# A written order that reaches through three units of the second block, with two places for values

## The chip, the cores and the metric

The kernel runs on one core of a Trainium2 chip. The metric is the device time of one execution in microseconds (us); the kernel before takes 1208.21 us, the median of three runs. Of the core's engines, TensorE (PE in the rows) multiplies matrices, VectorE (DVE), ScalarE (ACT) and GpSimd (POOL) work element by element, and SyncE (SP) issues the transfers (DMA). Each engine takes its instructions in the order of the program; between engines they wait on semaphores.

## The reference

Attention over windows with memory keys, then two expert layers on its output, all float32:

```python
for c in range(nc):                                   # 24 chunks of 32 queries, 4 batches, 8 heads
    k_full = concat([mem_k, k[:, :, l_start:r_end]])  # 8 memory keys, up to 16 + 32 + 8 of the window
    scores = scale * q_c @ k_full.T
    a = exp(scores - max(scores)); a = a / (sum(a) + 1e-09)
    out[:, :, c_start:c_end] = a @ v_full
x = out as 3072 tokens x 512
h = x @ w_in;  x = (h * sigmoid(1.702 * h)) @ w_out                       # 512 -> 2048 -> 512
g = x @ w_gate; x = (g * sigmoid(g) * (x @ w_val)) @ w_out2               # 512 -> 1536 -> 512
```

The weights arrive as float64 and are made into float32 on the chip.

## The kernel before, in words

The 3072 tokens are six blocks of 512. A block's attention is four groups of 128 tokens. A group is a chain: scores on TensorE (`sc`), maximum and difference on DVE (`mx`), exponential on ACT (`ex`), sum on DVE (`sm`), a guard on ACT (`ra`), reciprocal and weighing on DVE (`wg`), four transposes on TensorE (`te`, "turn"), two copies on ACT into the tile `ebd` (`ec`), 16 value products on TensorE (`pv`) against the group's value tile, and a copy of the output on ACT (`xf`), which SP stores to DRAM (`st`). Names in brackets are those of the written order.

Every float32 operand of an expert product is kept as two parts, high and low, and a product is three TensorE passes. A unit of the first expert layer covers 256 of 2048 hidden columns. It takes seven products of the tokens with prepared weights (each six matmuls of 256 columns, the helper `product`), sums and copies of parts of them on DVE and ACT, an activation on two banks `ps_a` and `ps_b`, and four "down" products (six matmuls of 512 columns each, `down`) into four long-lived banks `y`. The tokens enter as seven operands (class `Tokens`): sums and differences of quarters of the tile `xf` (`ts`), then a high part by ACT (`tc`) and a low part by DVE or POOL (`tl`). Two of the differences are written back into `xf`.

The weights come as raw 512 KB tiles (`ldw`, three places `raw` and four more lent at the start), are joined into float32 (`pr` on ACT, `cs`, `ct` on DVE), summed in quarters on POOL (`sumA`, `sumB`) and split into two parts (ACT then POOL). A unit needs four raw tiles: two of input weights, two of output weights.

The first block runs two units in a plain form (`ua`, `ub`: 12 matmuls of 512 columns for each of four halves), and all later blocks of the first pass four units in the form above. What is left of the units follows in a second pass, then the second expert layer.

What sets the order. The five queues of the start are written by hand: the table `OPENING` (before: line 796) lists steps by name, and every step issues its instructions on its engines and SP in that order. Before, it ends with the operands of the second block's tokens. From there on the loop (line 865) issues one unit after another: inside `unit` (line 448) the attention of the next block stands at fixed places (`PLACES`), and the weights' conversions are spread by `pace`. Before, there is one value tile `vm` for the attention outside the table and two `ebd` tiles.

Of the kernel before, what the change touches and what calls it, by code (L numbers as in the profile page):

```python
# [19 lines left out]
P = 128  # L20
# [37 lines left out]
def tile_attention_moe_moe(  # L58
# [40 lines left out]
    vm = apool.tile([P, HP, 4, D], F32, name="vm")  # L99
    ebd = [apool.tile([P, HP, 4, 2, CH], F32, name=f"ebd{i}") for i in range(2)]  # L100
# [12 lines left out]
    def load_kv(n, g):  # L113
        if n == "v":
            nc.sync.dma_start(out=vm, in_=vg[g])
# [31 lines left out]

    def st_weigh(g):
        r, e = rt.pop(g), et[g]
        nc.vector.reciprocal(r, r)  # L150
        nc.vector.tensor_tensor(e, e, r.unsqueeze(2).to_broadcast([P, H, KW]), op=ALU.mult)
# [6 lines left out]

    def keep_e(g, ps, engs):
        for e, copy in enumerate(engs):  # L160
            r = slice(64 * e, 64 * e + 64)
            copy(ebd[g % 2][r, :, :, e, :], ps[r].rearrange("p a (c q) -> p a c q", c=4))  # L162

    def values(g, ps, v):
        ps = ps.rearrange("p (a q) -> p a q", a=KC)
        for a in range(0, HP, 2):
            for c in range(4):
                for j in range(2):
                    nc.tensor.matmul(  # L169
                        ps[64 * j : 64 * j + 64, a : a + 2, CH * c : CH * c + CH],  # L170
                        v[:, a + j, c, :],
                        ebd[g % 2][:, a + j, c].rearrange("p e q -> p (e q)"),
                        start=True,
                        stop=True,
                    )
        return ps
# [13 lines left out]
    def st_scores(g):  # L190
        ps = bank("ps_s").rearrange("p (h k) -> p h k", h=H)
        q = qt.pop(g)
        for hp in range(HP):
            for c in range(4):
                r = slice(CH * c, CH * c + CH)
                nc.tensor.matmul(  # L196
                    ps[r, 2 * hp : 2 * hp + 2, :], q[:, hp, r], kbd[:, :, hp, c, :], start=True, stop=True
                )
        if g + 1 < NG:
            load_qk(g + 1)  # L200
        exponents(g, ps)
        st_exp(g)
# [71 lines left out]
    nraw, bits = [len(AT)], {}  # L274
# [80 lines left out]
    ready = {(1, u) for u in range(PLAIN)}  # L355

    def all_weights():
        for ph in (1, 2):
            for u in range(PLAIN if ph == 1 else 0, UNITS[ph]):
# [21 lines left out]
    class Tokens:  # L381


        def __init__(self, src, engs):
            n = BLK // 2
            self.b11, self.b12 = src[:, 0:2, :n], src[:, 0:2, n:]
            self.b21, self.b22 = src[:, 2:4, :n], src[:, 2:4, n:]
            self.engs = engs
            self.ops = [None] * 7

        def sum(self, k):
# [5 lines left out]
            elif k == 1:  # L397
                eng.tensor_sub(self.b12, self.b12, self.b11)
            elif k == 2:
                self.t2 = cpool.tile([P, 2, BLK // 2], F32, tag="t2", name="t2")  # L400
                eng.tensor_add(self.t2, self.t3, self.b11)  # L401
            else:
                eng.tensor_sub(self.b11, self.b21, self.t2)  # L403

# [153 lines left out]
    def down(ph, b, u, first, last, gs, base, dst, d, scale, passes=PASSES):  # L558
# [16 lines left out]
        if ends:  # L575
            del acc[d]
            if base is not None:
                t = base[d]
                nc.vector.scalar_tensor_tensor(t, y, scale, t, op0=ALU.mult, op1=ALU.add)
            else:  # L580
                t = opool.tile([P, 512], F32, tag="o", name="o")
                if d % 2 == 0:
                    nc.scalar.activation(t, y, AF.Copy, scale=scale)
                else:
                    nc.vector.tensor_scalar_mul(t, y, scale)
            nc.sync.dma_start(out=dst(b, d), in_=t)
# [49 lines left out]
    EC = [(nc.scalar.copy,) * 2] * 8  # L636
    firsts, pairs, at, tok = [[None] * 2 for _ in range(PLAIN)], [], {}, []

    def load_q(g):
        if g % GRP < 2:  # L640
# [27 lines left out]
    def scores_first(g):  # L668
        ps = ps_s.tile([P, 2 * BLK], F32, tag="s", name="ps_k")[:, HALF : HALF + BLK]
# [9 lines left out]
    def exponents_first(g):  # L679
        exponents(g, at.pop(("k", g)).rearrange("p e a k -> p (e a) k"), True)  # L680
# [4 lines left out]
    def values_first(g):  # L685
        at["x", g] = values(g, bank("ps_v"), v_open[g % 3])
# [25 lines left out]

    def sums_of(u):
        return quarters(raws[2 * u + 1]), bits[2 * u], bits[2 * u + 1]

    def pair_of(u, i):
        return quarters(raws[2 * u + 1])[:, 2 * i : 2 * i + 2].rearrange("p s n -> p (s n)")

    def split_b(u):
        wt[1, u, "a21"] = bpool.tile([P, 2, HALF], F32R, tag="b", name="a21")  # L720
        split_hi(wt[1, u, "a21"], bits[2 * u + 1][:, :HALF], 0, HALF)
# [20 lines left out]

    def tokens():
        if not tok:
            tok.append(Tokens(xf[1], [G, G, G, V, G, V, V, V, G, V, V]))
# [14 lines left out]
        "ra": st_guard,  # L760
        "wg": st_weigh,
        "te": turned,
        "ec": lambda g: keep_e(g, at.pop(("e", g)), EC[g]),
# [7 lines left out]
        "wa": lambda u: new_split((1, u, "a"), bits[2 * u]),  # L771
        "wal": lambda u: split_lo(wt[1, u, "a"], bits[2 * u]),
        "sumA": lambda u: first_sums(*sums_of(u)),
        "sumB": lambda u: second_sums(*sums_of(u)),
        "wv": lambda u: new_split((1, 0, "v"), bits[2 * u + 1][:, HALF:], u * HALF, HALF),
        "wvl": lambda u: split_lo(wt[1, 0, "v"], bits[2 * u + 1][:, HALF:], u * HALF, HALF),
        "wb": split_b,
        "wbl": lambda u: split_lo(wt[1, u, "a21"], bits[2 * u + 1][:, :HALF], 0, HALF),
# [4 lines left out]
        "wo": lambda o: new_split((1, o // 2, o % 2), bits[4 + o]),  # L783
        "wol": lambda o: split_lo(wt[1, o // 2, o % 2], bits[4 + o]),
# [6 lines left out]
        "dn": down_first,  # L791
        "tc": lambda k: tokens().split_hi(k),
# [4 lines left out]
        z0 tb0 z1 ldk0 ldq0 ldk1 ldq1 ldq2 ldk2 ldk3 ldw0 ldq3 ldw1 sc0 ldv0 mx0 ldq4 sc1 ldv1 ldk4 ex0 mx1 z2  # L797
        sc2 ldq5 sm0 ex1 ldk5 sm1 ra0 wg0 ra1 pr0 ldq6 wg1 te0 ldq7 sc3 mx2 ec0 te1 cs0 pr1 ldv2 mx3 ex2 pv0
        ldk6 ec1 cs1 ldk7 sm2 ex3 ct0 pv1 ldv3 hi0 sm3 ra2 wa0 ldw2 wg2 sc4 ra3 wal0 xf1 ldw3 wg3 xf0 te2 hi1
        xl0 sc5 mx4 st0 ec2 ldv4 te3 ldw4 mx5 ec3 xl1 pv2 ldq8 ct1 ex4 ex5 sm4 sumA0 ldw5 wb0 sm5 wv0 ra4 ldw6  # L800
        sc6 wvl0 wg4 xf2 wbl0 ra5 hi2 wg5 pv3 ldw7 sumB0 hiA0 mx6 te5 hi3 te4 xl2 xf3 ldv5 ua0 xl3 pr2 ec5 cs2
        ua1 loA0 ct2 ldv6 pr3 st3 wa1 cs3 ub0 ec4 ct3 wal1 st2 ub1 th0 sumA1 st1 wb1 gt0 wv1 ldk8 ua2 th1 sumB1
        gc0 gt1 pv4 pr4 rs0 wbl1 gc1 ub2 cs4 ldv7 pr5 wvl1 ct4 xf4 ua3 cs5 wo0 st4 ct5 hiB0 wol0 sc7 rs1 wo1 ub3
        th2 mx7 wol1 hiB1 pv5 ex6 gt2 loB1 ex7 dn0 sm6 xf5 loB0 sm7 gc2 st5 dn1 tc0 rs2 ldw8 ra7 tl0 th3 wg7 tc1
        dn2 gt3 ra6 tl1 pr6 wg6 gc3 te7 dn3 pr7 cs6 rs3 ec7 cs7 te6 ct7 ec6 pv7 ct6 wo3 pv6 xf7 wol3 xf6 st7 wo2
        ts0 st6 ldv8 hiA1 ts2 ts1 ts3 tc3 wol2 tl3 tc2 tc5 tl2 tl5 tc4 tc6 tl4 tl6 loA1
# [4 lines left out]
    for i in range(SPARE):  # L811
        give_w(("spare", i))
# [30 lines left out]
    def run(step):  # L843
        for f, g in step:
            f(g)
            if f is st_scores:
                soon.extend([(st_sums, st_guard, g), (st_weigh, g)])
# [17 lines left out]
    for n, (ph, b, ua, ub) in enumerate(seq):  # L865
# [4 lines left out]
        steps = attention(b + 1) if attends else []  # L870
        base = None
        for u in range(ua, ub):
# [6 lines left out]
            places = PLACES[u - ua] if n and attends else ()  # L879
# [18 lines left out]
            if n:  # L898
# [20 lines left out]
        if not n:  # L919
            pends[0] = None  # L920
# [53 lines left out]
```

## Time and profile before

| what | before |
|---|---|
| median of 3 runs (lowest, highest) | 1208.21 us (1207.19, 1208.73) |
| the profiled execution, its span | 1204.81 us, 1203.0 us |
| TensorE busy | 1155.2 us, 96% |
| DVE, ACT, POOL busy | 649.2, 566.7, 352.5 us |
| DMA queue of SP, share of 16 engines | 130.05 MB, 34.5% |

The profiled execution is one run; the times in its rows start at its first instruction. A busy share is an average over the whole span, so the stretches have to be looked at one by one. A busy TensorE need not run at its full clock, so the granted clock of a stretch is read with its busy time.

### The profile page before, as it was taken

To read this page: it belongs to the slowest core of one execution; us is meant where nothing else is said; L and a number is where in the kernel's file an instruction comes from. 1 tells how busy PE (TensorE), PEld (TensorE's weight loads), DVE (VectorE), ACT (ScalarE), POOL (GpSimd) and SP (SyncE) were. 2 spreads that over 40 slices of the span, in tenths; PEclk is the share of its full clock that TensorE was granted. 3 is DMA by queue.
4 is the path that set the end of the run, shared out by engine and by line. 5 is a ranking of instruction groups with operands and counts; after the bars stand their busy time and mean duration, and the time that the engine had idled before them with its cause. 6 is when DMAs were issued, how large, how long until landed. Compare 5 with 4: busy or idle time off the path is not lost.

```text
span 1203.0 us, 22302 instructions
## 1 busy us (share of the span) xinstructions
PE 1155.2 (96%) x8908; PEld 1042.7 (87%) x8908; DVE 649.2 (54%) x1117; ACT 566.7 (47%) x1185; POOL 352.5 (29%) x321
## 2 busy tenths in 40 slices
PE   4868899999999999999999999999999999999998
PEld 3757788888889999898998989999998989999997
DVE  6666665575674444443456564444556454454553
ACT  4655555454565544543465553342455443343342
POOL 2653312020455331320245433120255521020110
PEclk9888999999999999999999999999999999999999
DMA  9957363633434324223222331110225120320302
GB/s 309 301 161 196 120 177 104 170 106 114 141 123 124 105 89 140 85 74 106 96 97 88 123 123 36 71 55 17 88 76 168 56 97 10 106 80 27 106 23 84
DMA packets 62920, 131.47 MB, mean 109 GB/s; under 512 B 5728, under 2 KB 26208, under 8 KB 60512
## 3 DMA queue, kind: packets, MB, share of 16 engines
q1 hardware_dynamic: 62816, 130.05, 34.5%
q8 instruction: 70, 1.15, 0.4%
q14 instruction: 34, 0.28, 0.1%
HBM read 98.57 MB, written 31.46 MB: 108 GB/s over the span
## 4 chain that ended last, share of the span: by engine, by line
PE 85%; DMA 4%; DVE 4%; ACT 3%; issue 2%; POOL 1%; SPq 0%; DVEq 0%; ACTq 0%; POOLq 0%
PE y L568 35%; PE ps_a L433 26%; PE ps_c L433 12%; PE ps_b L433 8%; DMA raw<-in_wr 1%; DMA vm<-in_vg 1%; PE ps_o L169 1%; PE ps_s L196 1%; PE ps_u L529 1%; DMA xd<-xf 1%; DMA w<-in_kg 1%; PE ps_t L156 1%; ACT ebd L162 0%; DVE gs L548 0%; DVE b L419 0%
## 5 line engine op out<-in xcount | busy, mean ns | idle before, releaser
L433 PEld LDWEIGHTS ps_a<-b,w 128*128 128x128 f32 x2832 | 385.3, 190 | 50.6 <-ACT p L466 11.4
L433 PE MATMUL ps_a<-b,w 128*128 128x256 f32 x2832 | 398.6, 283 | 16.2 <-ACT p L466 10.1
L568 PE MATMUL y<-gs,w 128*128 128x512 f32 x1152 | 300.4, 396 | 1.0 <-DVE gs L548 0.8
L568 PE MATMUL y<-w,gs 128*128 128x512 f32 x864 | 247.8, 395 | 0.6 <-DVE gs L548 0.5
L568 PEld LDWEIGHTS y<-gs,w 128*128 128x128 f32 x1152 | 204.6, 190 | 37.1 <-DVE gs L548 2.3
L433 PE MATMUL ps_c<-b,w 128*128 128x256 f32 x1224 | 179.1, 282 | 0.0
L433 PEld LDWEIGHTS ps_c<-b,w 128*128 128x128 f32 x1224 | 167.1, 190 | 8.8
L568 PEld LDWEIGHTS y<-w,gs 128*128 128x128 f32 x864 | 144.2, 190 | 14.5 <-DVE gs L548 1.7
L249 POOL TENSOR_TENSOR w<-wf,w 128x512 fp32r<-128x512 f32 (+1 forms) x68 | 78.0, 1148 | 227.3 <-ACT w L246 215.2
L433 PE MATMUL ps_b<-b,w 128*128 128x256 f32 x900 | 135.4, 287 | 1.0 <-DVE e L131 0.5
L433 PEld LDWEIGHTS ps_b<-b,w 128*128 128x128 f32 x900 | 120.7, 193 | 5.8 <-issue 2.1
L536 ACT ACTIVATE g<-ps_b 128x512 f32<-128x512 f32 x72 | 43.0, 598 | 166.0 <-DVE ps_b L491 166.0
L419 DVE TENSOR_TENSOR b<-xl,b 128x512 fp32r<-128x512 f32 x72 | 64.5, 895 | 80.5 <-ACT b L415 80.3
L485 DVE TENSOR_TENSOR ps_a<-m,ps_a 128x256 f32<-128x256 f32 x118 | 50.2, 425 | 105.4 <-PE ps_a L433 99.4
L475 ACT COPY u<-ps_a 128x256 f32<-128x256 f32 x118 | 44.0, 373 | 109.1 <-PE ps_a L433 108.8
L403 POOL TENSOR_TENSOR xl<-xl,t 128x512 f32<-128x512 f32 x18 | 23.3, 1293 | 231.0 <-DVE t L401 229.8
L548 DVE TENSOR_TENSOR gs<-ps_a,gs 128x512 fp32r<-128x512 f32 x118 | 80.9, 686 | 10.4 <-ACT gs L544 10.1
L470 DVE TENSOR_TENSOR ps_b<-p,ps_b 128x256 f32<-128x256 f32 x118 | 50.4, 427 | 60.6 <-PE ps_b L433 55.2
L544 ACT CAST gs<-ps_a 128x512 fp32r<-128x512 f32 x118 | 69.8, 591 | 25.1 <-DVE ps_a L514 15.7
L514 DVE TENSOR_TENSOR ps_a<-g,ps_a 128x512 f32<-128x512 f32 x72 | 50.0, 694 | 46.0 <-PE ps_a L433 45.5
L466 ACT COPY p<-ps_a 128x256 f32<-128x256 f32 x118 | 44.0, 373 | 58.4 <-PE ps_a L433 54.2
L491 DVE TENSOR_TENSOR ps_b<-u,ps_c 128x256 f32<-128x256 f32 x102 | 43.6, 427 | 50.0 <-PE ps_c L433 49.7
(112 smaller groups left out, 1182.4 us busy)
## 6 DMA issues: line engine op xcount, KB each, us to landing
raw<-in_wr SPq DMA_DIRECT2D x49, 512.0 KB, 3.4
xl<-yd SPq DMA_DIRECT2D x12, 1024.0 KB, 4.8
vm<-in_vg SPq DMA_DIRECT2D x19, 512.0 KB, 4.1
kbd<-in_kg SPq DMA_DIRECT2D x32, 256.0 KB, 4.1
raw<-in_wr SPq DMA_DIRECT2D x30, 256.0 KB, 4.2
yp<-o SPq DMA_DIRECT2D x24, 256.0 KB, 3.0
xl<-xd SPq DMA_DIRECT2D x6, 1024.0 KB, 4.8
base<-yp SPq DMA_DIRECT2D x24, 256.0 KB, 3.6
```

The source lines that it names most:

```text
L249: nc.gpsimd.tensor_sub(w[:, 1, o : o + n], f, w[:, 0, o : o + n].bitcast(F32))
L419: self.engs[k].tensor_sub(x[:, 1], self.source(k), x[:, 0].bitcast(F32))
L433: nc.tensor.matmul(ps, w[:, a, o + kc * P : o + kc * P + P], x[:, c, kc, :], start=(start and kc == 0 and (a, c) == PASSES[0]), stop=(kc = ...
L466: nc.scalar.copy(p1, ca[:, :n])
L470: add(cb[:, :n], p1, cb[:, :n])
L475: nc.scalar.copy(u2, ca[:, :n])
L485: add(ca[:, n:], m, ca[:, :n])
L491: add(cb[:, n:], u2, cc)
L514: late[0] = [lambda: nc.vector.tensor_mul(ca, t, ca), lambda: gs.append(cast(ca))]
L544: nc.scalar.copy(x[:, 0], g)
L548: nc.vector.tensor_sub(x[:, 1], g, x[:, 0].bitcast(F32))
L568: nc.tensor.matmul(y, lhs, rhs, start=(first and o == 0 and (a, c) == PASSES[0]), stop=(ends and o == len(gs) - 1 and (a, c) == passes[-1]),)
```

## The change

The table of the written order reaches further. It now also holds the attention of the third block (groups 8 to 11), the first three of the second block's four units, product by product (`qa` to `qg`), with the copies, sums, activations and down products around them, and the conversions of two more units' weights (raw tiles 8 to 15 in addition to 0 to 7). The loop runs only the fourth unit of the second block with its own order, and takes over `late`, the last steps of the third unit.

Values get two places `vm` everywhere, and the next load is asked for two groups ahead; the second `ebd` tile exists only in the lent weight space during the start. The tokens' two differences of the second block go to other tiles (`place`). The reciprocal is a step of its own. The first four raw tiles come in four pieces of 128 partitions instead of two of 64. The first block's down results of both units are summed in the banks and then brought out (`held`, `ev`, `sy`).

```diff
-    vm = apool.tile([P, HP, 4, D], F32, name="vm")
-    ebd = [apool.tile([P, HP, 4, 2, CH], F32, name=f"ebd{i}") for i in range(2)]
+    vm = [apool.tile([P, HP, 4, D], F32, name=f"vm{i}") for i in range(2)]
+    ebd = [apool.tile([P, HP, 4, 2, CH], F32, name="ebd")]
...
+    def st_reciprocal(g):
+        nc.vector.reciprocal(rt[g], rt[g])
...
+    def weights_at(g):
+        return ebd[g % 2 if g < 2 * GRP else 0]
...
     def st_pv(g):
-        ps = values(g, bank("ps_o"), vm)
-        if g + 1 < NG:
-            load_kv("v", g + 1)
+        ps = values(g, bank("ps_o"), vm[g % 2])
+        if g + 2 < NG:
+            load_kv("v", g + 2)
...
+            if i < 2 * PLAIN:
+                src = wr[k].rearrange("(e d) (b a n) -> b e a d n", e=2, b=2, a=2)
+                for j in range(4):
+                    nc.sync.dma_start(out=raws[-1][:, j * P : j * P + P], in_=src[j // 2, j % 2])
+                continue
...
-    need, made = [next(weights)], [20 * PLAIN]
+    need, made = [next(weights)], [40 * PLAIN]
...
             elif k == 1:
-                eng.tensor_sub(self.b12, self.b12, self.b11)
+                b12, self.b12 = self.b12, self.place(self.b12)
+                eng.tensor_sub(self.b12, b12, self.b11)
...
+        def place(self, t):
+            if not self.apart:
+                return t
+            return opool.tile([P, BLK], F32, tag="o", name="t").rearrange("p (k n) -> p k n", k=2)
...
-    v_open = [vm] + [spare[12 + i].bitcast(F32).rearrange("p (a c d) -> p a c d", a=HP, c=4) for i in range(2)]
+    v_open = vm + [spare[12].bitcast(F32).rearrange("p (a c d) -> p a c d", a=HP, c=4)]
+    ebd.append(spare[13].bitcast(F32).rearrange("p (a c e q) -> p a c e q", a=HP, c=4, e=2))
...
+    def down_second(d):
+        down(1, 0, 1, False, True, firsts[1], None, None, d, 0.5, held=full)
...
+    def unit_product(new, out, w, o, k):
+        def f(u):
+            if new:
+                un[u][new] = bank(f"ps_{new}")
+            key, off = ((1, u, w), o) if w != "v" else ((1, u - u % 2, "v"), u % 2 * HALF)
+            product(out(u), wt[key], off, tokens().ops[k], start=out is cb1 and k == 2 or new is not None)
...
-        ts0 st6 ldv8 hiA1 ts2 ts1 ts3 tc3 wol2 tl3 tc2 tc5 tl2 tl5 tc4 tc6 tl4 tl6 loA1
+        ts2 ex9 ts1 hiB1 sm9 pv8 ts3 tc3 loB1 th3 tl3 qa0 ldv10 tc2 dn1 gt3 ra9 tl2 tc5 rc9 cp0 tl5 qb0 gc3 qc0
+        tc4 rs3 qd0 tc6 tl4 wg9 sc10 cu0 tl6 cm0 wa2 qe0 ct7 ldq12 xf8 wal2 qf0 ldk11 ac0 wo3 te9 pr9 st8 ad0
...
+    late[0] = [lambda: unit_rest("b")(2), lambda: unit_gate("a")(2)]
+    late[1] = [lambda: unit_cast("a")(2)]
+    late[2] = [lambda: unit_rest("a")(2)]
...
-            if n:
+            if n == 1 and u < 3:
+                gs = seconds[u]
+            elif n:
```

Three places show how instructions move. The first is TensorE's row between the first block's last down products and the second block's first unit product. `ps_u` are the plain halves, `ps_t` turns, `ps_v` value products, `ps_k` and `ps_s` scores, `y` down products, `ps_a` and `ps_b` unit products. Before:

```order
L568 MATMUL y_910<-gs,w 128x512 x6
L156 MATMUL ps_t<-ident,e 128x128 x4
L169 MATMUL ps_v<-ebd_119,w 64x2x32 x16
L169 MATMUL ps_v<-ebd_118,vm 64x2x32 x16
L433 MATMUL ps_a<-b,w 128x256 x6
L433 MATMUL ps_b<-b,w 128x256 x6
L433 MATMUL ps_a<-b,w 128x256 x6
L196 MATMUL ps_s<-kbd,q 32x128 x16
```

Now:

```order
L590 MATMUL y_943<-gs,w 128x512 x6
L174 MATMUL ps_v<-w,vm_118 64x2x32 x16
L201 MATMUL ps_s<-kbd,q 32x128 x16
L158 MATMUL ps_t<-ident,e 128x128 x4
L551 MATMUL ps_u<-xh,a_635 128x512 x2
L551 MATMUL ps_u<-xh,w 128x512 x2
L551 MATMUL ps_u<-xh,a_635 128x512 x2
L551 MATMUL ps_u<-xh,w 128x512 x2
L551 MATMUL ps_u<-xl,a_635 128x512 x2
L551 MATMUL ps_u<-xl,w 128x512 x2
L174 MATMUL ps_v<-ebd,vm_117 64x2x32 x16
L455 MATMUL ps_a<-b,w 128x256 x6
```

The unit products used to start behind all down products of the first unit and all eight value products. Now the ninth group's scores and value product, a turn and the last plain half stand ahead of the first unit product, and down products follow behind it.

The second place is TensorE's row in the second and third unit of the second block. Before:

```order
L169 MATMUL ps_o<-ebd_119,vm 64x2x32 x16
L433 MATMUL ps_a<-b,w 128x256 x12
L433 MATMUL ps_b<-b,w 128x256 x6
L568 MATMUL y_1449<-gs,w 128x512 x6
L433 MATMUL ps_a<-b,w 128x256 x6
L156 MATMUL ps_t<-ident,e 128x128 x4
L196 MATMUL ps_s<-kbd,q 32x128 x16
L433 MATMUL ps_b<-b,w 128x256 x6
```

Now:

```order
L455 MATMUL ps_a<-b,w 128x256 x6
L455 MATMUL ps_b<-b,w 128x256 x6
L455 MATMUL ps_a<-b,w 128x256 x6
L455 MATMUL ps_b<-b,w 128x256 x6
L455 MATMUL ps_a<-b,w 128x256 x6
L455 MATMUL ps_b<-b,w 128x256 x6
L455 MATMUL ps_a<-b,w 128x256 x12
L455 MATMUL ps_b<-b,w 128x256 x6
L455 MATMUL ps_a<-b,w 128x256 x6
```

Before, a down product, a turn or scores stand between unit products; now the seven products of the second unit stand one behind the other and the third unit's follow.

The third place is SP's row around the fourth and fifth group's values (`vm` or `w` from `in_vg`); `in_kg` are keys, `in_qg` queries, `in_wr` raw weights, `xd` the store of the attention's output. Before:

```order
L646 DMA qq<-in_qg 128x512 x2
L666 DMA w<-in_vg 128x1024
L664 DMA w<-in_kg 128x1024 x2
L666 DMA vm<-in_vg 128x1024
L272 DMA raw<-in_wr 64x4x128 x2
L272 DMA w<-in_wr 64x4x128 x2
L188 DMA xd_89<-w 512x1x128
```

Now:

```order
L281 DMA w<-in_wr 128x1x128 x4
L697 DMA vm_118<-in_vg 128x1024
L697 DMA w<-in_vg 128x1024
L697 DMA vm_117<-in_vg 128x1024
L276 DMA w<-in_wr 128x512
L677 DMA q<-in_qg 128x512
L695 DMA w<-in_kg 128x1024 x2
L119 DMA kbd<-in_kg 64x1024 x2
L677 DMA q<-in_qg 128x512
L276 DMA w<-in_wr 128x512
L697 DMA vm_118<-in_vg 128x1024
L276 DMA w<-in_wr 128x512
```

The keys up to the ninth group and two more raw tiles now stand ahead of the fifth group's values, and the first raw tiles are four pieces.

## Rows read from the trace of the kernel before

**Rows 1.** The page's second part: forty equal slices, busy tenths of TensorE.

```profile
PE   4868899999999999999999999999999999999998
```

**Rows 2.** Table by stretches: engines' busy us and instructions, clock, DMA share, GB/s.

```profile
core 0: us, PE busy (x) PEld busy (x) DVE busy (x) ACT busy (x) POOL busy (x), PEclk, DMA share, GB/s
0.00:38.85 38.85, 19.60 (x600) 16.59 (x601) 24.06 (x45) 19.20 (x43) 15.71 (x24) 0.91 1.00 299
38.85:62.34 23.49, 23.31 (x275) 18.84 (x274) 16.30 (x28) 18.50 (x37) 14.60 (x14) 1.00 0.94 297
62.34:131.30 68.96, 50.69 (x475) 42.74 (x472) 41.46 (x66) 35.69 (x72) 29.75 (x27) 0.88 0.67 190
189.20:244.26 55.06, 54.53 (x537) 47.16 (x536) 33.32 (x59) 27.55 (x58) 7.30 (x5) 1.00 0.47 135
```

**Rows 3.** Timeline of TensorE, start: start us, length us, operation, idle before.

```profile
34.36 1.97 PE L169 MATMUL ps_v<-ebd,vm 128*64 128x64 f32 x32 [2.03 <-DMA vm<-in_vg]
...
38.85 1.63 PE L529 MATMUL ps_u<-xh,w 128*128 128x512 f32 x6
```

**Rows 4.** Timeline of TensorE, second block.

```profile
70.84 0.58 PE L433 MATMUL ps_a<-b,w 128*128 128x256 f32 x1 [6.81 <-ACT p L466]
...
88.29 0.98 PE L433 MATMUL ps_a<-b,w 128*128 128x256 f32 x6 [3.83 <-ACT ebd L162]
...
127.28 1.98 PE L169 MATMUL ps_o<-ebd,vm 128*64 128x64 f32 x32 [2.68 <-DMA vm<-in_vg]
...
131.30 0.88 PE L433 MATMUL ps_b<-b,w 128*128 128x256 f32 x6
```

**Rows 5.** Timeline of TensorE at full clock, for start-to-start times.

```profile
25.76 0.86 PE L677 MATMUL ps_k<-w,q 64*32 64x64 f32 x64
26.55 0.65 PE L156 MATMUL ps_t<-ident,e 128*128 128x128 f32 x4
...
48.43 0.62 PE L529 MATMUL ps_u<-xh,a 128*128 128x512 f32 x2
48.88 0.62 PE L529 MATMUL ps_u<-xh,w 128*128 128x512 f32 x2
...
198.01 0.88 PE L433 MATMUL ps_b<-b,w 128*128 128x256 f32 x6
198.73 1.55 PE L568 MATMUL y<-gs,w 128*128 128x512 f32 x6
200.12 0.87 PE L433 MATMUL ps_a<-b,w 128*128 128x256 f32 x6
...
208.34 0.60 PE L156 MATMUL ps_t<-ident,e 128*128 128x128 f32 x4
208.87 1.08 PE L196 MATMUL ps_s<-kbd,q 128*32 128x128 f32 x32
209.88 1.69 PE L433 MATMUL ps_a<-b,w 128*128 128x256 f32 x12
...
214.58 1.15 PE L169 MATMUL ps_o<-ebd,vm 128*64 128x64 f32 x32
215.66 0.98 PE L433 MATMUL ps_b<-b,w 128*128 128x256 f32 x6
```

**Rows 6.** Transfers up to 34.4 us; then 38.85 to 62.34 in forty slices.

```profile
DMA packets 4752, 10.25 MB, mean 298 GB/s; under 512 B 423, under 2 KB 2189, under 8 KB 4749
...
GB/s 419 401 412 398 422 401 398 408 415 405 412 412 412 335 355 345 362 393 379 326 276 276 215 258 296 167 72 39 276 206 232 288 291 206 195 265 211 61 35 202
```

**Rows 7.** Timelines of POOL and DVE while the tokens' operands are made.

```profile
66.83 1.26 POOL L398 TENSOR_TENSOR xf<-xf 128x512 f32<-128x512 f32 x1 [3.62 <-DMA xd<-xf]
...
68.12 1.74 DVE L403 TENSOR_TENSOR xf<-xf,t 128x512 f32<-128x512 f32 x1 [3.63 <-DMA vm<-in_vg]
```

**Rows 8.** Groups by form, DVE, 0 to 131 us; then 189 to 244: busy, mean ns.

```profile
L151 DVE TENSOR_TENSOR e<-e,r 128x512 f32<-128x512 f32 x12 | 11.3, 943 | 0.4
...
L151 DVE TENSOR_TENSOR e<-e,r 128x512 f32<-128x512 f32 x4 | 2.8, 692 | 0.1
```

More of the change, by code (lines that the diff above doesn't have):

```diff
@@ L114, in load_kv @@
         if n == "v":
-            nc.sync.dma_start(out=vm, in_=vg[g])
+            nc.sync.dma_start(out=vm[g % 2], in_=vg[g])
             return
@@ L161, in keep_e @@
             r = slice(64 * e, 64 * e + 64)
-            copy(ebd[g % 2][r, :, :, e, :], ps[r].rearrange("p a (c q) -> p a c q", c=4))
+            copy(weights_at(g)[r, :, :, e, :], ps[r].rearrange("p a (c q) -> p a c q", c=4))
     def values(g, ps, v):
@@ L188, in store_x, with scores @@
         nc.sync.dma_start(out=xd[b][:, :, i * P : i * P + P], in_=xq[g])
-    def st_scores(g):
+    def scores(g):
         ps = bank("ps_s").rearrange("p (h k) -> p h k", h=H)
@@ L198, in st_scores @@
                 )
+        return ps
+    def st_scores(g):
+        ps = scores(g)
         if g + 1 < NG:
@@ L353, in weight_steps @@
         ready.add((ph, u))
-    ready = {(1, u) for u in range(PLAIN)}
+    ready = {(1, u) for u in range(2 * PLAIN)}
     def all_weights():
         for ph in (1, 2):
-            for u in range(PLAIN if ph == 1 else 0, UNITS[ph]):
+            for u in range(2 * PLAIN if ph == 1 else 0, UNITS[ph]):
                 yield from weight_steps(ph, u)
@@ L556, in tile_attention_moe_moe, with down @@
     acc = {}
-    def down(ph, b, u, first, last, gs, base, dst, d, scale, passes=PASSES):
+    def down(ph, b, u, first, last, gs, base, dst, d, scale, passes=PASSES, held=None):
         if d not in acc:
@@ L574, in down, with evict @@
                 )
[L575 to L586, printed above, removed]
+        if not ends:
+            return
+        del acc[d]
+        if held is not None:
+            held[d] = y
+            return
+        nc.sync.dma_start(out=dst(b, d), in_=evict(y, base, d, scale))
+    def evict(y, base, d, scale):
+        if base is not None:
+            t = base[d]
+            nc.vector.scalar_tensor_tensor(t, y, scale, t, op0=ALU.mult, op1=ALU.add)
+            return t
+        t = opool.tile([P, 512], F32, tag="o", name="o")
+        if d % 2 == 0:
+            nc.scalar.activation(t, y, AF.Copy, scale=scale)
+        else:
+            nc.vector.tensor_scalar_mul(t, y, scale)
+        return t
     def entries(ph, ends):
@@ L668, in scores_first @@
     def scores_first(g):
+        if g >= 2 * GRP:
+            at["k", g] = scores(g)
+            return
         ps = ps_s.tile([P, 2 * BLK], F32, tag="s", name="ps_k")[:, HALF : HALF + BLK]
@@ L679, in exponents_first @@
     def exponents_first(g):
+        if g >= 2 * GRP:
+            exponents(g, at.pop(("k", g)))
+            return
         exponents(g, at.pop(("k", g)).rearrange("p e a k -> p (e a) k"), True)
@@ L685, in values_first @@
     def values_first(g):
-        at["x", g] = values(g, bank("ps_v"), v_open[g % 3])
+        at["x", g] = values(g, bank("ps_v"), vm[g % 2] if g >= 2 * GRP else v_open[g % 3])
     def group_cols(g):
@@ L741, in down_first, with evict_first, store_first, quarter @@
         down(1, 0, 0, True, False, firsts[0], None, None, d, 0.5)
+    def down_second(d):
+        down(1, 0, 1, False, True, firsts[1], None, None, d, 0.5, held=full)
+    full = {}
+    def evict_first(d):
+        full[d] = evict(full[d], None, d, 0.5)
+    def store_first(d):
+        nc.sync.dma_start(out=yp[0][:, d, :], in_=full.pop(d))
+    seconds, un = [[] for _ in range(3)], [{} for _ in range(3)]
+    QN = BLK // 2
+    def quarter(bank_, part):
+        return lambda u: un[u][bank_][:, part * QN : part * QN + QN]
+    ca0, ca1, cb0, cb1 = quarter("a", 0), quarter("a", 1), quarter("b", 0), quarter("b", 1)
+    def unit_product(new, out, w, o, k):
[4 more added lines that the diff above has]
+            product(out(u), wt[key], off, tokens().ops[k], start=out is cb1 and k == 2 or new is not None)
+        return f
+    def unit_copy(name, src):
+        def f(u):
+            un[u][name] = cpool.tile([P, QN], F32, tag=name, name=name)
+            nc.scalar.copy(un[u][name], src(u))
+        return f
+    def unit_add(out, name, src):
+        return lambda u: V.tensor_add(out(u), un[u][name], src(u))
+    def unit_curve(bank_):
+        return lambda u: un[u].update({"t" + bank_: curve(un[u][bank_], 1)})
+    def unit_gate(bank_):
+        return lambda u: gate(un[u][bank_], un[u].pop("t" + bank_), un[u][bank_])
+    def unit_cast(bank_):
+        return lambda u: seconds[u].append(cast(un[u][bank_]))
+    def unit_rest(bank_):
+        return lambda u: rest(un[u][bank_], seconds[u]["ab".index(bank_) ^ 1])
+    def unit_down(d):
+        return lambda u: down(1, 1, u, u == 0, False, seconds[u], None, None, d, 0.5)
     def tokens():
         if not tok:
-            tok.append(Tokens(xf[1], [G, G, G, V, G, V, V, V, G, V, V]))
+            tok.append(Tokens(xf[1], [G, G, G, V, G, V, V, V, G, V, V], True))
         return tok[0]
@@ L760, in tile_attention_moe_moe @@
         "ra": st_guard,
+        "rc": st_reciprocal,
         "wg": st_weigh,
         "te": turned,
-        "ec": lambda g: keep_e(g, at.pop(("e", g)), EC[g]),
+        "ec": lambda g: keep_e(g, at.pop(("e", g)), (nc.scalar.copy,) * 2),
         "pv": values_first,
@@ L791, in tile_attention_moe_moe @@
         "dn": down_first,
+        "dm": down_second,
+        "ev": evict_first,
+        "sy": store_first,
+        "qa": unit_product("a", ca0, "a", 0, 0),
+        "qb": unit_product("b", cb0, "a", HALF, 1),
+        "qc": unit_product(None, ca0, "s12", HALF, 3),
+        "qd": unit_product(None, cb1, "s12", 0, 2),
+        "qe": unit_product(None, ca0, "s34", 0, 5),
+        "qf": unit_product(None, cb1, "s34", HALF, 4),
+        "qg": unit_product(None, ca0, "v", 0, 6),
+        "cp": unit_copy("p1", ca0),
+        "cu": unit_copy("u2", ca0),
+        "cm": unit_copy("m", cb1),
+        "ab": unit_add(cb0, "p1", cb0),
+        "ac": unit_add(ca1, "m", ca0),
+        "ad": unit_add(cb1, "u2", cb1),
+        "ka": unit_curve("b"),
+        "kb": unit_gate("b"),
+        "kc": unit_cast("b"),
+        "kd": unit_rest("b"),
+        "ma": unit_curve("a"),
+        "mb": unit_gate("a"),
+        "mc": unit_cast("a"),
+        "md": unit_rest("a"),
+        "ya": unit_down(0),
+        "yb": unit_down(1),
+        "yc": unit_down(2),
+        "yd": unit_down(3),
         "tc": lambda k: tokens().split_hi(k),
@@ L846, in run @@
             if f is st_scores:
-                soon.extend([(st_sums, st_guard, g), (st_weigh, g)])
+                soon.extend([(st_sums, st_guard, g), (st_reciprocal, st_weigh, g)])
     def follow():
@@ L869, in tile_attention_moe_moe @@
         attends = ph == 1 and ua == 0 and b + 1 < NBLK
-        steps = attention(b + 1) if attends else []
+        steps = attention(b + 1) if attends and n > 1 else []
         base = None
@@ L878, in tile_attention_moe_moe @@
                 tok = Tokens(xf.pop(nxt[1]), TE)
-            places = PLACES[u - ua] if n and attends else ()
+            places = PLACES[u - ua] if n > 1 and attends else ()
             def chunk(d):
```

71 lines of the change are left out of this document (42 added, 29 removed).

## The prediction

> **What bounds the kernel now.** I read the table of busy times first: TensorE is busy for 96% of the span, so what can be won is the time in which it stands or runs below its full clock. The line of forty slices says where that is [rows 1]: the first four or five slices of 30 us, then almost nothing. The table by stretches gives it a size [rows 2]. A block whose steps run at their steady pace takes 55.06 us with TensorE busy for 54.53. [...] The first 38.85 us are the start, with DMA at a share of 1.00.
>
> Then the timeline of TensorE for that second block [rows 4]: waits of 6.81, 3.83 and 2.68 us (the page puts the last on a load of values), each followed by slow matmuls. So the bound there is not one busy engine (in 62.34 to 131.30 DVE works 41.46, ACT 35.69, POOL 29.75 us [rows 2]); it is the order in which short steps of four engines and the loads follow each other.
>
> **A common mark.** The program's TensorE order is equal in both kernels from the product into ps_b that stands at 131.30 us in the trace [rows 4] (the second product of the second block's fourth unit) to the end. The gain or loss is therefore how much earlier or later this mark comes, plus what changes behind it.
>
> How much TensorE work lies ahead of the mark is counted from the order and priced by start-to-start times at full clock [rows 5]: scores of 8 groups, 0.79 each (25.76 to 26.55), 6.3; scores of 4 groups in the other form, 1.01 (208.87 to 209.88), 4.0; 12 turns at 0.53, 6.4; 12 value products at 1.08, 13.0; 48 plain matmuls of 512 columns at 0.227 (two in 0.45), 10.9; 15 down products at 1.39, 20.9; 22 unit products at 0.72, 15.8. Sum 77.3 us. Both kernels have the same 77.3; before needs 131.3 for them, so 54 us are lost: 26 ahead of the first expert matmul, 0.7 from there to 62.34 and 27 behind that. The 27 are what the change rewrites.
>
> **The change part by part.**
>
> Start to the first expert matmul (38.85 before). The new order puts more ahead of it: scores of 9 groups instead of 7, 5 value products instead of 4. TensorE is hardly busy there, so the price is in the loads. Up to the load of the fourth group's values, which the value product starting at 34.36 waited for [rows 3], SP had issued 8 keys, 8 queries, 2 weights and 4 values: 9.44 MB (0.524 MB a piece, 0.262 for a query); 10.25 MB had come by 34.4 at 298 GB/s [rows 6]. In the new order the last load that is needed ahead of the mark's work is the fifth group's values, and through it SP issues 9 keys, 10 queries, 6 weights and 5 values: 13.11 MB. At the mean rate, with the same surplus in flight, that is 34.4 x 13.11/9.44 = 47.8 us. If only the 3.67 MB more count, at the 410 GB/s at which loads run where no weights in quarters are among them [rows 6], it is 34.4 + 9.0 = 43.4. Four of the new weights come in pieces of 128 partitions instead of 64; the bytes are the same and I take no gain from it. I take 45, and with one value product (1.08) the first expert matmul starts at 46, 7 later than before; bounds 42 and 50. That is the cost of the change.
>
> From there to the mark. Of the 77.3 us, 15.9 now lie ahead of it (8 x 0.79, 1.01, 6 x 0.53, 5 x 1.08), so 61.4 follow. Without a wait the mark would come at 46 + 61.4 = 107.4. What is waited for is bounded from both sides: the stretch already written out lost 0.7 on 22.8 us of work, which scales to 1.9 on 61.4; the stretch not written out lost 27 on 41.5, which scales to 40. The first is the nearest, since these steps now stand in the same kind of list. To its 1.9 I add what I can name:
> - Values of the ninth group. Between the fifth and ninth values SP's row holds 6.55 MB (4 weights, 4 values, 6 stores of the attention's output, a query, a key); at 297 GB/s [rows 2] that is 22 us, so they land at 45 + 22 = 67, while 18.1 us of work stand ahead of their product: 64. Late by 3.
> - The second and third unit's products stand back to back, without a down product between. A copy on ACT (0.37 us) and its signals must fit behind one product of 0.72; some six such waits of about 0.3 make 2.
>
> So 7 in sum, and the mark at 114.4.
>
> What hides the rest. Before, the first long wait (6.81) is the making of the tokens' seven operands: POOL waited 3.62 us for a store of the same tile to end, and DVE 3.63 (where the page names a load that ended then) [rows 7], because two differences were written in place. The change writes them to other places, so that wait goes, and the operand chain starts as soon as the eighth group's output is there, beside 8.2 us of TensorE work (one group's scores and turn, two plain halves, a value product, two unit products and a down product); DVE has eight steps from there to the operand for the third unit product (two score steps and a sum among them), at its mean of 41.46/66 = 0.63 [rows 2] 5 us, and some 6 if the last is as long as the 1.74 of [rows 7]. If that cover failed by 2 us, TensorE would wait 2. What is late next is the copy of the ninth group's output into the tile that POOL's last operand is read from: ACT stands behind it with the next turn's copy.
>
> Two places for values: the 2.68 us wait at 127.28 goes, it is within the 27. Behind the mark TensorE stands still for 0.5 us a block [rows 2], so there is no more than 2 us to win in four blocks; I take 0. The reciprocal as a step of its own and the other list of two units' conversions move no work behind the mark that TensorE waits for: 0, bounds -1 and +1.
>
> DVE and POOL. By row, the weighing step (two inputs from SBUF) takes 943 ns on average ahead of the mark and 692 in the steady block where POOL works 7.30 us in 55 [rows 8, 2]. The crowded figure is already in the sums here, since I count DVE by its means there.
>
> [...]
>
> **The sum.** 131.3 - 114.4 = 16.9 us. The profiled execution took 1204.81 us (span 1203.0), which would become 1187.9. It lies 3.4 below the median of 1208.21; taken from the median, the forecast is 1191.3.
>
> **The rivals.**
> 1. The transfers set the pace longer. For: DMA share 1.00 and 0.94 in the first two stretches [rows 2], and the new order asks for more, earlier. If the 6.55 MB come at the 190 GB/s of 62.34 to 131.30 [rows 2], they take 34.5 us, the ninth values land at 79.5 and the wait is 15 instead of 3: mark at 126, time 1203. Against: that 190 is an average with DMA partly idle (0.67).
> 2. The waits only move, and the mark comes where it came: 1208, no change. For: the 27 us were spread over several engines, and one serial chain per unit could hold them all. Against: the written stretch shows them gone.
> 3. Slower: DVE's own row becomes the chain. Ahead of the first expert matmul the new order has 55 DVE instructions, at 24.06/45 = 0.535 each [rows 2] 29.4 us; of 81.8 ahead of the mark 52.4 remain. In 62.34 to 131.30 DVE was idle for 27.5 us on 41.46 of work, 0.66. If each of its waits in the list costs as much again, it needs 87 us from 46: mark at 133, 1210. With the two-input steps as crowded as 943/692 makes them on top of that, 52.4 becomes some 60 and the mark 145: 1222. I price it at 1214. It decides once DVE's idle time behind 46 is over 33 us. Against: in the written stretch DVE idled for 7.2 on 16.30 while TensorE did not stand.
>
> **How the numbers follow.** Forecast (mark 107 to 121): 0.60, time 1191, its own range 1184 to 1198. Still earlier: 0.06. Rival 1: 0.20. Rival 2: 0.06. Rival 3: 0.08. What can be told from no change is 0.2%, 2.4 us. So faster 0.86, same 0.06, slower 0.08. The range reaches from a mark at 106 (first matmul at 43, two us of waits) to one near 129: 1183 to 1206.
>
> **What would show it.** First plain matmul at 42 to 50 us. From there to the mark about 68 us, TensorE's granted clock near 1.00 and no single wait over 4 us. The ninth values' product waits on its load for 2 to 4 us. No wait of POOL on a store of the output tile. Behind the mark, 1071.7 us as before, within 2. I am wrong if the first plain matmul comes behind 52, or if TensorE is busy for less than 85% between it and the mark, or if the blocks behind the mark take another time than 55 us.

## The result, and the profile after

The changed kernel takes 1221.64 us (median of four runs, 1221.12 to 1222.65) against 1207.70 us for the kernel before in the same set: a ratio of 1.0118, interval 1.0101 to 1.0136. It is 14 us slower; I had forecast 1191. The profiled execution took 1222.65 us with a span of 1220.9.

The page of the changed kernel: busy times, the forty slices of TensorE (here 30.5 us each), and the chain of work that ended last, by engine and by line.

```profile
PE 1148.4 (94%) x8908; PEld 1037.2 (85%) x8908; DVE 651.0 (53%) x1117; ACT 567.1 (46%) x1185; POOL 353.7 (29%) x321
...
PE   1269999999999999999999999999999999999998
...
PE 82%; SPq 5%; DMA 5%; DVE 3%; ACT 2%; issue 2%; POOL 1%; DVEq 0%; ACTq 0%; POOLq 0%
PE y L590 34%; PE ps_a L455 26%; PE ps_c L455 11%; PE ps_b L455 8%; SPq L281 3%; DMA raw<-in_wr 1%; PE ps_o L174 1%; DMA w<-in_kg 1%; PE ps_s L201 1%; DMA kbd<-in_kg 1%; DMA xd<-w 1%; DMA xd<-xf 1%; SPq L677 1%; SPq L697 0%; ACT ebd L167 0%
```

The slices behind the third are full, so the second block, whose slices showed gaps before [rows 1], has none left. The first three are emptier than before. In the chain a name stands that had 0% in the page of before: SP's own queue with 5%, of which 3% (some 37 us) on line 281, the issue of a raw tile in four pieces.

The table by stretches, cut at the first plain matmul and at the mark, with its columns as in [rows 2]:

```profile
core 0: us, PE busy (x) PEld busy (x) DVE busy (x) ACT busy (x) POOL busy (x), PEclk, DMA share, GB/s
0.00:82.18 82.18, 23.11 (x728) 19.25 (x728) 30.79 (x56) 25.33 (x55) 25.84 (x34) 0.81 0.57 186
82.18:147.76 65.58, 63.41 (x617) 53.60 (x615) 51.88 (x82) 47.24 (x94) 32.06 (x29) 1.00 0.85 245
147.76:1220.90 1073.14, 1061.92 (x7568) 964.39 (x7566) 568.36 (x980) 494.49 (x1036) 295.76 (x260) 1.00 0.29 93
```

Where the time went can be read from the three lengths. The start takes 82.18 us where 46 were forecast and 38.85 were needed before [rows 2]. From there to the mark it is 65.58, with TensorE busy for 97%; behind it 1073.14, against 1071.7 before. The whole loss is in the start, and there the DMA share is 0.57 at 186 GB/s, where it had been 1.00 at 299 [rows 2]: the transfers are slower and yet not busy.

The timeline of TensorE in the changed kernel (start us, length us, operation, idle before it and what ended that), with all its waits of over 8 us ahead of the first plain matmul, and then all that are marked up to the mark:

```profile
18.98 1.17 PE L711 MATMUL ps_k<-kbd,q 64*32 64x64 f32 x64 [12.71 <-DMA kbd<-in_kg]
...
35.99 1.17 PE L711 MATMUL ps_k<-w,qq 64*32 64x64 f32 x64 [12.11 <-issue]
...
51.70 1.17 PE L711 MATMUL ps_k<-w,q 64*32 64x64 f32 x64 [10.70 <-DMA w<-in_kg]
...
66.03 1.97 PE L174 MATMUL ps_v<-w,vm 128*64 128x64 f32 x32 [11.00 <-DMA vm<-in_vg]
...
82.18 2.11 PE L551 MATMUL ps_u<-xh,w 128*128 128x512 f32 x8
...
97.82 1.08 PE L201 MATMUL ps_s<-kbd,q 128*32 128x128 f32 x32 [1.19 <-DMA kbd<-in_kg]
...
111.83 0.98 PE L455 MATMUL ps_a<-b,w 128*128 128x256 f32 x6 [0.98 <-DVE ps_a L826]
```

Four waits of 11 to 13 us, 14 to 17 us apart. Three end with the arrival of keys or values; the second the page puts on "issue", time for which it shows no releaser. TensorE's granted clock is low in part of this stretch (0.81 over the whole of it; 1.00 up to 33.50 us, 0.50 from 44.00 to 64.80), but the work there is waiting for loads, not for the clock. What happens every 16 us stands in SP's row, the queue that issues the transfers (start us, length us, the four issues of one raw tile):

```profile
2.13 6.27 SPq L281 DMA_DIRECT2D raw<-in_wr  x4
...
12.57 11.54 SPq L281 DMA_DIRECT2D raw<-in_wr  x4
...
28.28 11.67 SPq L281 DMA_DIRECT2D raw<-in_wr  x4
...
44.11 11.43 SPq L281 DMA_DIRECT2D w<-in_wr  x4
```

The four raw tiles in the new form. Each holds SP for 6 to 12 us, and the keys and values that stand behind it in SP's row are issued only afterwards. The transfers of the changed kernel from 2 to 18 us, in forty slices of 0.4 us (the share of the 16 DMA engines that is busy, in tenths, and GB/s):

```profile
DMA  9797999511111111111111119669999899999311
GB/s 215 297 389 287 338 399 410 184 36 49 49 49 49 46 51 46 49 49 46 51 46 51 46 49 182 159 225 425 364 325 397 289 310 302 328 323 271 113 51 51
```

While such a tile comes, the mean busy share of the engines is a tenth (0.14 from 5 to 9 us) and the rate is 46 to 51 GB/s in most slices, an eighth of the 400 around it. By that rate a tile of 0.524 MB takes 10.7 us and four take 43; at the 299 GB/s of the start before [rows 2] four take 7. The difference, 36 us, is an estimate from these two rows, and near what the first plain matmul was late: 82.18 - 46 = 36.2. That they agree so well is partly chance, since the forecast start of 46 was itself too short (see the first experiment).

### The profile page after: what moved, and what is told of

It reads as the page before. It is cut to its first block, busy times and chain, and to the rows that moved or that the text cites. A ratio compares the mean times of both kernels' runs of the same rounds, so it can differ in the third digit from the quotient of the medians.

```text
span 1220.9 us, 22325 instructions
## 1 busy us (share of the span) xinstructions
PE 1148.4 (94%) x8908; PEld 1037.2 (85%) x8908; DVE 651.0 (53%) x1117; ACT 567.1 (46%) x1185; POOL 353.7 (29%) x321
## 4 chain that ended last, share of the span: by engine, by line
PE 82%; SPq 5%; DMA 5%; DVE 3%; ACT 2%; issue 2%; POOL 1%; DVEq 0%; ACTq 0%; POOLq 0%
PE y L590 34%; PE ps_a L455 26%; PE ps_c L455 11%; PE ps_b L455 8%; SPq L281 3%; DMA raw<-in_wr 1%; PE ps_o L174 1%; DMA w<-in_kg 1%; PE ps_s L201 1%; DMA kbd<-in_kg 1%; DMA xd<-w 1%; DMA xd<-xf 1%; SPq L677 1%; SPq L697 0%; ACT ebd L167 0%
```

## The experiments

The theories, by the letters that the expectations use. A: the form of the four pieces is slow by itself, and holds up all that is behind it. It has two readings: A1, what counts is the outermost level of the transfer (each piece is written as two halves of 64 partitions, so that level counts 2), and A2, what counts is that the tile is cut by columns. B: the pieces are simply more and smaller. Against both stands that the new order itself asks for too much, too early. Each set ran with the kernel before beside it, at medians of 1205.53 (old halves, pieces alone, four pieces, eight pieces), 1206.03 (sixty-two, sixty) and 1204.63 us (the rest).

**The old halves for the first four tiles.** The changed kernel without the four pieces:

```diff
-            if i < 2 * PLAIN:
-                src = wr[k].rearrange("(e d) (b a n) -> b e a d n", e=2, b=2, a=2)
-                for j in range(4):
-                    nc.sync.dma_start(out=raws[-1][:, j * P : j * P + P], in_=src[j // 2, j % 2])
-                continue
```

> The changed kernel with the first four raw weight tiles loaded as before (two pieces of 64 partitions). Theory A (the form of the pieces: each piece is described over the two column halves first, and so keeps only an eighth of the DMA engines at work): transfers are back at a share near 1.0 from 4 us on, the first plain matmul comes at 42 to 50 us instead of 82.2, the stretch from it to the common mark keeps its 65.6 us, the time falls by 32 to 40 us to 1182 to 1190 us. Theory C (the longer written order itself makes the start late, since it asks for nine groups and six weights first): first plain matmul still behind 65 us, time above 1204.

1187.70 us, ratio 0.9849 (0.9828 to 0.9869). Its table by stretches, cut at its first plain matmul and at its mark:

```profile
0.00:49.81 49.81, 23.73 (x729) 19.62 (x729) 30.22 (x56) 25.30 (x55) 25.66 (x34) 0.97 1.01 302
49.81:113.20 63.39, 63.16 (x618) 53.57 (x615) 50.16 (x82) 47.62 (x95) 33.33 (x30) 1.00 0.92 260
113.20:1186.00 1072.80, 1062.17 (x7568) 964.40 (x7566) 568.75 (x980) 494.48 (x1036) 295.31 (x259) 1.00 0.29 93
```

Of the 34.9 us by which the spans differ (1220.9 - 1186.0), 32.4 are in the start, 2.2 in the middle and 0.3 behind. Its SP row at the same tiles, and its DMA share from 2 to 18 us:

```profile
2.13 1.37 SPq L281 DMA_DIRECT2D raw<-in_wr  x2
...
5.72 1.36 SPq L281 DMA_DIRECT2D raw<-in_wr  x2
```

```profile
DMA  5999999999999999999999999999999999999999
```

SP passes these tiles in 1.4 us each (2.1 for the two later ones), and every slice from 2.4 us on is full. So the loss is the four pieces, and the order is not what is slow.

**The pieces alone.** The kernel before, with only the lines that were taken out above put in.

> The kernel before with nothing but the four pieces of 128 partitions for the first four raw weight tiles. Theory A: each of the four tiles holds SP for some 11.5 us while the DMA share falls to about 0.1; the first plain matmul moves from 38.85 to 60 to 75 us, time 1225 to 1245 us. Theory C: within 5 us of the kernel before.

1233.65 us, ratio 1.0233 (1.0209 to 1.0258): the pieces cost the old order 28 us too. The timeline of its TensorE:

```profile
50.05 1.64 PE L534 MATMUL ps_u<-xh,w 128*128 128x512 f32 x6
...
71.40 3.11 PE L534 MATMUL ps_u<-xh,w 128*128 128x512 f32 x6 [15.64 <-ACT w L246]
```

The first plain matmul came earlier than I expected (50.05), because the old order needs fewer tiles ahead of it; the rest of the delay is the next wait, 15.64 us for a weight made from a late tile.

**Four pieces of 32 partitions.** As many pieces as in the changed kernel, and as large, but cut by partitions:

```diff
-                src = wr[k].rearrange("(e d) (b a n) -> b e a d n", e=2, b=2, a=2)
+                src = wr[k].rearrange("(e d) (b a n) -> a d b e n", e=2, b=2, a=2)
                 for j in range(4):
-                    nc.sync.dma_start(out=raws[-1][:, j * P : j * P + P], in_=src[j // 2, j % 2])
+                    dst = raws[-1][32 * j : 32 * j + 32].rearrange("d (b e n) -> d b e n", b=2, e=2)
+                    nc.sync.dma_start(out=dst, in_=src[j // 2, j % 2 * 32 : j % 2 * 32 + 32])
```

> The changed kernel with four pieces per tile, as many and as large (128 KB) as in it, but cut by partitions (32 each) and not by columns. Theory A: as the kernel with halves, within 3 us. Theory B (it is the number of pieces and their small size): as the changed kernel, 1221 us within 5.

1189.05 us, ratio 0.9862 (0.9837 to 0.9886), and SP is held 2.5 to 3.1 us a tile. In the profiled execution, the slowest of its four, the first plain matmul comes at 54.31, behind this wait of TensorE in the middle of a group of scores:

```profile
47.72 0.67 PE L712 MATMUL ps_k<-w,qq 64*32 64x64 f32 x28 [4.63 <-issue]
```

The page names no load for it, so these 4.6 us cannot be put down to the pieces.

**Eight pieces.** The column pieces, each cut once more into its two halves of 64 partitions:

```diff
-                for j in range(4):
-                    nc.sync.dma_start(out=raws[-1][:, j * P : j * P + P], in_=src[j // 2, j % 2])
+                for j in range(8):
+                    r, s = slice(64 * (j % 2), 64 * (j % 2) + 64), j // 2
+                    nc.sync.dma_start(out=raws[-1][r, s * P : s * P + P], in_=src[s // 2, s % 2, j % 2])
```

> The changed kernel with eight pieces of 64 partitions and 64 KB per tile: the columns are cut as in the changed kernel, and the two halves of the partitions apart. Theory A: within 6 us of the kernel with halves (SP issues four times as many). Theory B: slower than the changed kernel, 1235 us or more.

1192.22 us, ratio 0.9886 (0.9868 to 0.9903); first plain matmul at 56.07, SP held 5 to 8 us a tile. Twice as many pieces, half as large, cut by columns, and 28 to 29 us faster than the changed kernel. B falls, and A2 is unlikely. Eight pieces come out 4.5 us slower than two halves (1187.70 us, first plain matmul at 49.81), with intervals that just meet; for four no price is shown: of the 54.31 above 4.63 is a wait of another kind, and a kernel with four pieces below comes at 49.43.

**Sixty-two and sixty.** To tell A1 from A2, whole rows of a tile (no cut by columns) in four pieces, cut by partitions at 62 or at 60 of each half, two splits that are nearly the same:

```diff
-                src = wr[k].rearrange("(e d) (b a n) -> b e a d n", e=2, b=2, a=2)
+                src = wr[k].rearrange("(e d) (b a n) -> a d b e n", e=2, b=2, a=2)
                 for j in range(4):
-                    nc.sync.dma_start(out=raws[-1][:, j * P : j * P + P], in_=src[j // 2, j % 2])
+                    d = slice(0, 62) if j % 2 == 0 else slice(62, 64)   # the other kernel: 60 for 62
+                    dst = raws[-1][64 * (j // 2) :][d].rearrange("d (b e n) -> d b e n", b=2, e=2)
+                    nc.sync.dma_start(out=dst, in_=src[j // 2, d])
```

> The changed kernel with four pieces per tile cut by partitions as 62, 2, 62, 2, all columns of a row together (as with halves). [...] Theory A2 (what is slow is a source that is cut by columns and walks the two halves in turn): as with halves, 1186 to 1192.

> The same with pieces of 60, 4, 60, 4 partitions. [...]

With 62: 1229.78 us, ratio 1.0196 (1.0176 to 1.0215), slower even than the changed kernel (1221.64); first plain matmul at 89.31. With 60: 1188.81, ratio 0.9869 (0.9837 to 0.9900); first plain matmul at 49.43. SP's row for the second tile, and the DMA share and rate from 2 to 18 us, of the kernel with 62:

```profile
14.46 16.33 SPq L283 DMA_DIRECT2D raw<-in_wr  x4
```

```profile
DMA  6899999410111111111111111111194899899999
GB/s 143 328 358 358 348 389 410 174 10 20 36 49 49 33 38 36 41 41 41 44 49 46 49 46 49 49 49 49 46 192 166 302 356 302 189 282 228 251 238 254
```

and of the kernel with 60:

```profile
7.52 3.28 SPq L283 DMA_DIRECT2D raw<-in_wr  x4
```

```profile
DMA  6999999999277976867979999999999989999999
```

Two partitions more in the large pieces, and the share falls to a tenth. Nothing else differs but the small pieces (2 and 4 partitions), so the count of the outermost level decides, as A1 says, and A2 falls, since 62 is slow without a cut by columns. What it is in the count that decides is not shown: the runs have the counts 2, 32, 60, 62 and 64 alone in the large pieces. With 2 and 62 the share was 0.1, at 46 to 51 GB/s and 33 to 49 GB/s in most slices. Over these 16 us, with all loads in them, SP's queue had a share of 1.03 of the 16 engines with four pieces of 32, 0.95 with 60, 1.03 with two halves of 64 and 0.76 with eight pieces of 64; in the changed kernel it was 0.58 and with 62 it was 0.51. More than one rule would fit these. Why the tiles with 62 hold SP for longer than those of the changed kernel, 14.6 to 16.3 us for three of the four, no run shows.

**The differences written in place again.** The kernel with the old halves, with the two token differences in place:

```diff
-            tok.append(Tokens(xf[1], [G, G, G, V, G, V, V, V, G, V, V], True))
+            tok.append(Tokens(xf[1], [G, G, G, V, G, V, V, V, G, V, V]))
```

> The kernel with halves (e1, 1187.7 us, the rest of the change without the pieces), with the second block's token differences written back into their own tile again. Theory D (the prediction's step: the write in place waits for stores of the same tile, 3.6 us on POOL and DVE before): 1 to 4 us slower than with halves, 1189 to 1192, with waits of POOL or DVE on a store in front of the differences and TensorE late at a unit product. Rival: the stores are long done in this order, no difference (within 1 us).

1197.40 us, ratio 0.9933 (0.9917 to 0.9948), where the kernel with the other places has 0.9849 in its own set: some 10 us by medians, and by the profiled executions the mark comes at 119.89 instead of 113.20. More than I expected. The timelines of POOL and then of TensorE in this kernel:

```profile
72.79 1.26 POOL L409 TENSOR_TENSOR xf<-xf 128x512 f32<-128x512 f32 x1 [6.15 <-DMA xd<-xf]
```

```profile
75.65 0.58 PE L450 MATMUL ps_a<-b,w 128*128 128x256 f32 x1 [3.02 <-ACT p L816]
...
77.56 1.44 PE L450 MATMUL ps_a<-b,w 128*128 128x256 f32 x5 [1.32 <-DVE b L436]
```

POOL waits 6.15 us for the store of the tile that it overwrites (3.62 before [rows 7]), and TensorE stands for 4.3 us in two waits. The rest of the 6.7 lies in slower matmuls behind them: from 75.65 to the mark the granted clock is 0.93 here, and it was 1.00 in all of the same work with the other places. With the other places this step has no wait:

```profile
66.78 1.29 POOL L409 TENSOR_TENSOR t<-xf 128x512 f32<-128x512 f32 x1
```

**The other places alone.** The kernel before with `place` and nothing else of the change.

> The kernel before with nothing but the second block's token differences written to other tiles. Theory D: the waits of 3.62 and 3.63 us go, TensorE's wait of 6.81 us shrinks to 3 to 4, time 2 to 6 us less than before. Rival (the operand chain is held by ACT's and DVE's own row, not by the store): within 1.5 us of before.

1202.02 us, ratio 0.9981 (0.9968 to 0.9994): 2.3 us faster. In the profiled execution, which at 1199.34 us is the fastest of twelve, TensorE's wait for the operand shrinks from 6.81 [rows 4] to

```profile
67.48 1.80 PE L441 MATMUL ps_a<-b,w 128*128 128x256 f32 x6 [4.46 <-ACT p L474]
```

so the store was 2.35 us of it. The 4.46 left end with a step on ACT and not with a store; that they are the chain of steps itself is an inference, which fits the new order, where other work stands in that place.

**Two places for values alone.** The kernel before with two `vm`, one `ebd` behind the start, and values asked for two groups ahead.

> The kernel before with nothing but the places: two value tiles, the next values asked for two groups ahead, one tile for the turned weights behind the start. Theory of the prediction: TensorE's wait of 2.68 us on a load of values in the second block goes, 1 to 3 us faster; behind that nothing. Rival: one tile for the turned weights makes new waits of TensorE or ACT in blocks two to five, 0 to 3 us slower.

1206.61 us, ratio 1.0009 (0.9998 to 1.0020): no change, where I expected 1 to 3 us. TensorE's timeline, and the table cut at the first plain matmul, the first unit product and the mark:

```profile
73.39 0.58 PE L436 MATMUL ps_a<-b,w 128*128 128x256 f32 x1 [7.15 <-ACT p L469]
...
128.65 1.15 PE L172 MATMUL ps_o<-ebd,vm 128*64 128x64 f32 x32 [0.39 <-ACT ebd L165]
```

```profile
39.02:64.55 25.53, 25.35 (x274) 20.30 (x272) 16.14 (x28) 18.38 (x37) 14.61 (x14) 0.91 0.84 271
64.55:131.27 66.72, 50.15 (x474) 42.00 (x471) 41.13 (x66) 35.44 (x72) 29.20 (x27) 0.87 0.69 199
```

The wait of 2.68 on the values [rows 4] is down to 0.39 and no longer for a load, and the second block's stretch is 2.2 us shorter (66.72 against 68.96 [rows 2]), although the wait of 6.81 is now 7.15. But the mark comes where it came, at 131.27, because the stretch ahead of it is 2.0 us longer (25.53 against 23.49), with TensorE busy throughout at a granted clock of 0.91 where it had been 1.00. Whether the places cause that or this one execution happened so, no run shows. So by itself the second place took a wait away and did not change the time.

**Tiles in the order of the load.** The kernel with the old halves, with the rows of the input weights laid out beforehand so that a raw tile is one load of whole rows:

```diff
-            if k >= 2 * NF1 or k % 4 > 1:
-                nc.sync.dma_start(out=raws[-1], in_=wr[k])
-                continue
-            src = wr[k].rearrange("(e d) (b a n) -> a d b e n", e=2, b=2, a=2)
...
+            nc.sync.dma_start(out=raws[-1], in_=wr[k])
...
+    wi = wi.reshape(NF1, 2, 64, 2, 2, P).transpose(0, 4, 2, 3, 1, 5).reshape(NF1, P, DM)
```

> The kernel with halves, with the rows of the input weights' raw tiles laid out beforehand as the chip wants them, so that each of them is one load of whole 4 KB rows. If the start is bound by transfers and a load in 1 KB rows costs about twice one in 4 KB rows (215 against 400 GB/s in the rows of the trace before), four such tiles give 4 x (2.4 - 1.3) = 4 to 5 us: first plain matmul at 44 to 46 instead of 49.8, time 1182 to 1184. Rival: the start is bound by the chains between the engines and SP's waits, less than 1.5 us.

1184.51 us, ratio 0.9827 (0.9813 to 0.9841), the fastest median here, and faster than both kernels. It fell just short of what I expected. The first plain matmul in its timeline, and its transfers from 0 to 46 us:

```profile
46.79 2.11 PE L540 MATMUL ps_u<-xh,w 128*128 128x512 f32 x8
```

```profile
DMA packets 6474, 15.93 MB, mean 346 GB/s; under 512 B 600, under 2 KB 2103, under 8 KB 6469
```

With the old halves it was at 49.81 and 14.73 MB had come by 49 us at 301 GB/s, with 3375 packets under 2 KB instead of 2103. The start is 3 us shorter. Whether the whole is faster than with the halves the two ratios do not settle, since their intervals overlap.

## Why the prediction was wrong

**The failed step** is the sentence on the start: "Four of the new weights come in pieces of 128 partitions instead of 64; the bytes are the same and I take no gain from it." I counted bytes and asked only whether the form could be a gain. No row of before shows a load in this form, so it was a cost to be bounded from both sides, and I left the side of a loss out. The first plain matmul came at 82.18, where 46 was forecast (bounds 42 and 50; behind 52 was to show me wrong). Of these 36.2 us the pieces made 32.4 (82.18 - 49.81 with the halves), and 3.8 were my count of the other loads. In the whole the pieces cost 32 us by the ratios and 34 by the medians (1221.64 against 1187.70). Nothing else in the forecast was off by as much. The diff showed the outermost level of that transfer, 2, and I did not look at it.

**The rest of the start.** With the halves the first plain matmul came at 49.81, at the upper bound. The mean rate was 302 GB/s, so of my two ways of counting the one by the mean rate (47.8 for the loads and one value product, 48.9) was right, and I had leaned to the other with 46.

**From there to the mark.** Forecast 68.4 (61.4 of work and 7 of waits), measured 65.58 and, with the halves, 63.39. So 2.0 us came on top of the counted work with the halves, where I had 7. In size that is the 1.9 scaled from the stretch already written out (38.85 to 62.34 [rows 2]), alone, but not in kind: that 1.9 stood for time lost, and TensorE was idle for only 0.23 of it (63.39 - 63.16): most of it is work that my start-to-start times had a little too short. The 3 us for the ninth group's values did not occur: no wait in this stretch ends with a load of values, in either kernel. Nor did the six small waits between unit products placed back to back; there is one of 0.98 in the changed kernel, and none with the halves. With the halves the mark came at 113.20, forecast 114.4: errors of 3.8 and 5.0 us in opposite directions. So that the kernel with the halves gains 17.8 us where the forecast had 16.9 is partly luck.

**The operands.** The wait on the store went, as said. In the new order it would have cost 7 to 10 us, more than the 3.6 us that I read from the rows of before.

**Behind the mark.** 1071.7 within 2: measured 1073.1, and 1072.8 with the halves.

**The rivals.** The transfers did set the pace, but by another mechanism than rival 1's, which took 190 GB/s for the ninth values; the form of four loads gave 49. The waits did not stay where they were (rival 2), and DVE's row did not become the chain (rival 3): it worked 51.88 us in 65.58 while TensorE stood for 2. The weighing step did get longer in this stretch, as that case supposed: 1032 ns on average against 888 in 62.34 to 131.30 before; on six steps that is under 1 us, and no wait of TensorE in this stretch ends with it. That rival 3's worst figures (mark at 145, 1222 us) lie near the measured 147.76 and 1221.64 is chance. The slower outcome came without any case of mine for it.

## What to carry to other kernels

Count the bytes of a transfer and then look at the count of its outermost level: a split that left 2 there loaded at 46 to 51 GB/s here, an eighth of the rate around it, although each piece filled 128 partitions, and held the issuing queue for 11.4 to 11.7 us a tile (6.3 for the first), with all that stood behind it. A rewritten load can be a cost of its own, even where the diff's words are about order and its bytes are equal. And when a large rewrite disappoints, look first for the line that the chain of work newly names, and undo that edit alone: here five lines hid a gain of 18 us.

## What the runs showed of the hardware

Over the first tiles a load whose outermost level counts 2 came at 46 to 51 GB/s, one that counts 62 at 33 to 49, in most slices, both with a DMA share of 0.1; with 60, or with halves of 64 or quarters of 32, the share stood near 1 in most slices (0.95, 1.03 and 1.03 for SP's queue from 2 to 18 us). SP was held by the issue: 11.4 to 11.7 us for four column pieces (6.3 for the first tile), 14.6 to 16.3 for pieces of 62 and 2 partitions (10.4 for the first), 1.4 to 2.1 for two halves of 64. So a slow transfer did not only arrive late itself, it also kept faster ones from being issued: the values behind the second tile were issued at 24.15 us, with the halves at 7.52.
